# A decode step of attention and a gated unit on one core: the last V piece, the gate product and the weight pieces cut differently

## The chip, the core and the metric

The kernel runs on one core of one Trainium2 chip. The metric is device time in microseconds (us) of one execution. The engines are TensorE (PE, with its weight loads PEld), VectorE (DVE), ScalarE (ACT), GpSimd (POOL) and SyncE (SP); SP issues nearly all transfers, which 16 DMA engines carry out.

## What is computed

One token goes through a pre-norm attention with a cache and then through a gated unit, each with its residual:

```python
def _A_ref(x, k_cache, v_cache, wq, wo):        # x: 1 x 1 x 512
    q = (x @ wq) -> 32 heads of 128
    # 8 heads of K and V, 65536 rows of 128 each, shared by 4 heads of q
    p = softmax(q . k * 128 ** -0.5)
    return (p . v) -> 4096 values, @ wo          # 4096 x 512
def _B_ref(x, w_gate, w_up, w_down):             # 512 x 1792, 512 x 1792, 1792 x 512
    h = sigmoid(x @ w_gate) * (x @ w_up)
    return h @ w_down
h   = x + _A_ref(layernorm(x), ...)
out = h + _B_ref(layernorm(h), ...)
```

Everything is bf16. K and V are 134 MB each, the weights 14 MB.

## The kernel before

**Storage.** A ring in SBUF (`ring`) holds 32 chunks; a chunk is 16 rows of the cache per partition, 512 KB over 128 partitions. A head's K or V (32 chunks) is loaded in three pieces of 12, 8 and 12 chunks (`PIECES`, L228), each by one transfer on SP's queue (`load`, L323). Later the ring also takes w_gate, w_up and w_down (`AT`, L230). `ktw` holds transposed K and, at the end, the output weights wo.

**The loop over heads.** For each of 8 heads there are four blocks of 8 chunks. DVE transposes the chunks of K (L511), PE multiplies them with the query (scores, L430), DVE takes maxima, ACT takes exponentials (L557), and DVE transposes the result (L567). The sums over V of the head before run on PE between the scores: 16 rounds of eight matmuls (two chunks of V, four column tiles each; `pv`, L587, also L430), all adding into one PSUM bank (`PO`). Then ACT copies the bank out (L600), PE and ACT bring it into columns (L603, L606).

**How the order is made.** The engines' instruction lists are written out by hand with named dependencies (`Prog.op`, `Prog.dma`); a wait stands ahead of the instruction that needs it. PE's list is not unrolled. `pe_flow` (L669) is a small program of registers and branches. `sums` (label at L712, body L731 to L736) is one round of the V sums: `pv_regs` (L577) works out the addresses of the eight matmuls in registers, then eight matmuls follow, registers are moved on, and the counter `m` decides on another round. When `m` is 0 and `k` is not, PE jumps to the block `waits` (L718), which sets `m` to `k` and waits for the next V piece where one is due; from there it jumps back to `sums`. When both are 0, it goes on to `outs` (L740), the copy out. `away` (L672) writes a conditional jump to a block whose code stands behind the loop.

**The last head.** The V piece of chunks 20 to 31 comes in two transfers, chunks 20 to 27 and 28 to 31 (`LAST`, L318, L349). PE waits for the first (section V3, L711), runs four rounds, goes to `waits`, waits for the second (section VL, L729), and runs two rounds. While V's last pieces come in, PE works on wo for the first seven heads (`project7`, L636).

**The tail.** After the last head's copy out follow its part of wo (L632), a second layer norm (L804 to L811, hc at L805), 16 matmuls with w_gate and 16 with w_up (L818; four column tiles of 448 columns, four steps over the rows), tanh on ACT (L825), `sg2` on DVE (L826), the gate product `hh` (L828), its transpose `hhT` (L831), and 56 small matmuls with w_down: 14 rows of four column tiles (L836). Row r needs columns 32r to 32r + 31 of `hhT`. Two copies each on DVE and ACT (L842, L844) and one store (L846) end the kernel.

**Transfers of the tail.** SP issues, in this order: the last head's V pieces, w_gate in one piece (it waits for the first six rounds of the last head, since it lies where those chunks of V were), w_up in two (three steps of rows, then one; L316, L355), w_down in three (rows 0 to 7, 8 to 11, 12 to 13; L235, L360). Each piece has its own semaphore, and PE waits for it at its first matmul.

## Time and profile before

| | |
|---|---|
| median of 3 runs | 657.5 us (657.47 to 658.03) |
| the profiled execution | 657.62 us |
| its span in the profile | 656.2 us |
| PE busy | 436.0 us (66%) |
| DVE busy | 351.2 us (54%) |
| ACT busy | 42.8 us (7%) |
| read from memory | 282.33 MB, 430 GB/s over the span |
| granted TensorE clock, mean | 0.775 |

How to read it: the span is the time from the first to the last instruction that the profiler recorded; the execution's own time is 1.4 us longer. Busy times of engines overlap each other. A row of the timeline gives start and length in us, the engine, the line of the code, the operation, what it writes and reads, how many instructions were merged, and in brackets how long the engine had been idle before and who released it. "issue" is time in which the engine waited for nothing that the profile shows, and PEq is PE's sequencer, which also runs registers, branches and waits.

### The profile page before, as it was taken

To read this page: it belongs to the slowest core of one execution; us is meant where nothing else is said; L and a number is where in the kernel's file an instruction comes from. 1 tells how busy PE (TensorE), PEld (TensorE's weight loads), DVE (VectorE), ACT (ScalarE), POOL (GpSimd) and SP (SyncE) were. 2 spreads that over 40 slices of the span, in tenths; PEclk is the share of its full clock that TensorE was granted. 3 is DMA by queue.
4 is the path that set the end of the run, shared out by engine and by line. 5 is a ranking of instruction groups with operands and counts; after the bars stand their busy time and mean duration, and the time that the engine had idled before them with its cause. 6 is when DMAs were issued, how large, how long until landed. Compare 5 with 4: busy or idle time off the path is not lost.

```text
span 656.2 us, 6248 instructions
## 1 busy us (share of the span) xinstructions
PE 436.0 (66%) x2316; PEld 69.4 (11%) x1548; DVE 351.2 (54%) x436; ACT 42.8 (7%) x114; POOL 3.6 (1%) x17
## 2 busy tenths in 40 slices
PE   2698675838658457776676477594667856775855
PEld 1100010001001010010100110010100101001212
DVE  3498836847266645647258380674536572573102
ACT  1100200020000200011000200002000020002001
POOL 1000000000000000000000000000000000000000
PEclk9798688767689587796677676985877967877777
DMA  9999999999999999999999999999999999999998
GB/s 400 431 447 431 425 424 446 437 434 426 441 431 431 431 431 442 437 434 423 423 443 431 431 437 445 437 437 431 415 431 431 431 434 434 457 431 411 439 422 341
DMA packets 8386, 282.33 MB, mean 430 GB/s; under 512 B 961, under 2 KB 962, under 8 KB 1474
## 3 DMA queue, kind: packets, MB, share of 16 engines
q1 hardware_dynamic: 8354, 282.33, 99.6%
q10 hardware_dynamic: 32, 0.00, 0.0%
HBM read 282.33 MB, written 0.00 MB: 430 GB/s over the span
## 4 chain that ended last, share of the span: by engine, by line
DMA 65%; PE 19%; DVE 12%; issue 3%; ACT 1%; SPq 0%; PEldq 0%
DMA ring<-in_A_k_cache_dram 34%; DMA ring<-in_A_v_cache_dram 23%; PE PS L430 18%; DVE ktw L511 11%; DMA ring<-in_B_w_down_dram 6%; DMA ring<-in_A_wq_dram 2%; ACT P_sb L557 1%; DVE PT_sb L567 0%; DVE M_sb L518 0%; SPq L355 0%; PE PS L551 0%; PE PS L544 0%; PEldq L171 0%; SPq L360 0%; PE PS L572 0%
## 5 line engine op out<-in xcount | busy, mean ns | idle before, releaser
L511 DVE STREAM_TRANSPOSE ktw<-ring 128x1024 f32<-128x1024 f32 x256 | 292.4, 1211 | 170.5 <-DMA ring<-in_A_k_cache_dram 170.5
L430 PE MATMUL PS<-ktw 128*128 128x512 bf16 x1024 | 293.2, 438 | 114.8 <-DVE ktw L511 106.7
L430 PE MATMUL PS<-ring,PT_sb 128*32 x1024 | 102.7, 506 | 65.4 <-PEq L171 45.1
L430 PEld LDWEIGHTS PS<-ktw 128*128 x256 | 27.2, 106 | 370.4 <-issue 258.1
L600 ACT ACTIVATE po_sb<-PS,rl 128x512 bf16<-128x512 f32 x8 | 5.5, 687 | 522.2 <-PE PS L430 522.2
L430 PEld LDWEIGHTS PS<-ring,PT_sb 128*32 x1024 | 20.7, 116 | 144.3 <-issue 142.8
L518 DVE TENSOR_REDUCE M_sb<-PS 128x1 f32<-128x512 f32 x32 | 19.9, 684 | 20.0 <-PE PS L430 20.0
L546 DVE TENSOR_REDUCE gmj<-PS 1x4 f32<-1x128 f32 x8 | 2.2, 278 | 40.2 <-PE PS L544 40.2
L557 ACT ACTIVATE P_sb<-PS,negmax 128x512 bf16<-128x512 f32 x32 | 21.5, 685 | 0.3
L567 DVE STREAM_TRANSPOSE PT_sb<-P_sb 128x512 bf16<-128x512 bf16 x32 | 20.2, 688 | 1.7 <-ACT P_sb L557 1.7
L430 PE MATMUL PS<-ring,xz 128*8 x32 | 10.0, 490 | 3.6 <-DMA ring<-in_A_wq_dram 3.6
L616 DVE TENSOR_TENSOR Lw<-O,blk_of 128x896 bf16<-128x896 bf16 (+1 forms) x2 | 1.4, 682 | 19.9 <-ACT O L606 19.9
L544 PE MATMUL PS<-identf,gm 128*1 128x128 f32 x16 | 4.5, 380 | 5.5 <-issue 3.4
L551 PE MATMUL PS<-one_f,gmrep 1*128 1x1 f32 x16 | 4.7, 358 | 5.0 <-DVE gmrep L548 5.0
L574 DVE TENSOR_REDUCE lsum<-PS 128x1 f32<-128x4 f32 x8 | 1.3, 162 | 11.9 <-PE PS L572 11.9
L475 DVE STREAM_TRANSPOSE qt<-qh 32x512 bf16<-32x512 bf16 x1 | 0.7, 699 | 12.7 <-ACT qh L472 12.7
L430 PE MATMUL PS<-ktw,O 128*1 x26 | 7.5, 457 | 0.0
L557 ACT ACTIVATION_READ_ACCUMULATOR P_sb<-PS,negmax 128x1 f32 x32 | 6.5, 203 | 0.0
L603 PE MATMUL PS<-sel_bf,po_sb 128*128 128x4 bf16 x32 | 2.1, 170 | 6.3 <-ACT po_sb L600 6.3
L411 PE MATMUL PS<-xs,xpick 16*128 16x32 bf16 x1 | 0.2, 202 | 7.5 <-DMA xs<-in_A_x_dram 7.5
L572 PE MATMUL PS<-L_sb,lsel 128*128 128x4 f32 x16 | 2.5, 229 | 3.8 <-DVE PT_sb L567 3.8
L661 DVE COPY yr<-PS 1x512 f32<-1x512 f32 x1 | 0.7, 678 | 8.1 <-PE PS L659 8.1
(88 smaller groups left out, 71.6 us busy)
## 6 DMA issues: line engine op xcount, KB each, us to landing
ring<-in_A_k_cache_dram SPq DMA_DIRECT2D x16, 6144.0 KB, 25.4
ring<-in_A_v_cache_dram SPq DMA_DIRECT2D x15, 6144.0 KB, 25.7
ring<-in_A_v_cache_dram SPq DMA_DIRECT2D x9, 4096.0 KB, 30.6
ring<-in_A_k_cache_dram SPq DMA_DIRECT2D x8, 4096.0 KB, 24.7
ring<-in_A_wq_dram SPq DMA_DIRECT2D x1, 4096.0 KB, 12.3
ktw<-in_A_wo_dram SPq DMA_DIRECT2D x1, 3584.0 KB, 14.9
ring<-in_A_v_cache_dram SPq DMA_DIRECT2D x1, 2048.0 KB, 38.5
ring<-in_B_w_gate_dram SPq DMA_DIRECT2D x1, 1792.0 KB, 30.8
```

The lines of the kernel that those rows point to most:

```text
L430: return e.add_instruction(mybir.InstMatmult(name=nc.get_next_instruction_name(), engine=mybir.EngineType.PE, ins=[rhs, lhsT], outs=[e.low ...
L511: op("dve", lambda e, d=dst, sr=src: e.transpose(d, sr), deps, f"T{b}.{c}", to="T")
L518: op("dve", lambda e, u=u: e.tensor_reduce(M_sb[:, u % 4:u % 4 + 1], ps(u % NS, 0, 512), AX.X, ALU.max), [f"S{b}.{NC - NR + k}"], f"mx{u}" ...
L544: op("pe", lambda e: e.matmul(ps(MISC, 0, 128, 0, 1), lhsT=gm[:, :], rhs=identf[:, :], start=True, stop=True), [f"gm{h}"], f"gmT{h}", to="Q")
L546: op("dve", lambda e: e.tensor_reduce(gmj[:, :], ps(MISC, 0, 128, 0, 1).rearrange("p (i a c) -> p a i c", a=4, c=NC), AX.XY, ALU.max), [f" ...
L551: op("pe", lambda e: e.matmul(ps(MISC, 128, 129), lhsT=gmrep[0:1, :], rhs=one_f[0:1, 0:1], start=True, stop=True), [f"gmrep{h}"], f"neg{h}")
L557: op("act", lambda e, b=b: e.activation(P_sb[:, (b % 4) * 512:(b % 4 + 1) * 512], ps(b % NS, 0, 512), AF.Exp, bias=negmax[:, k:k + 1], sca ...
L567: op("dve", lambda e, b=b: e.transpose(PT_sb[:, (b % 4) * 512:(b % 4 + 1) * 512], P_sb[:, (b % 4) * 512:(b % 4 + 1) * 512]), [f"E{b}"], f" ...
L572: op("pe", lambda e: e.matmul(ps(MISC, 132, 136), lhsT=lsel[:, :], rhs=L_sb[:, :], start=True, stop=True), [f"PT{NR * h + NR - 1}"], f"l{h ...
L600: op("act", lambda e: e.activation(po_sb[:, :], ps(PO, 0, 512), AF.Copy, scale=rl[:, :]), [f"PV{h}.{NR - 1}", f"rl{h}"], f"po{h}", to="po")
L603: op("pe", lambda e, t=t: e.matmul(ps(OX, 0, 4), lhsT=po_sb[:, t * 128:(t + 1) * 128], rhs=sel_bf[:, 8 * t:8 * t + 8:2], start=(t == 0), s ...
L616: op("dve", lambda e: e.tensor_tensor(Lw[i][:, :].rearrange("p (j c) -> p j c", j=n), bass.AP(tensor=O2, offset=j0, ap=[[NQ, 128], [1, n], ...
```

## The change

Four things are cut differently.

1. V's chunks 28 to 31 of the last head come in two transfers, 28 to 29 and 30 to 31. PE runs four rounds, waits for 28 to 29, runs one round in the loop, comes to `waits` again, waits for 30 to 31, and runs the last round (`pv_last`) with its eight matmuls written out at fixed addresses. From there it jumps to `outs`.
2. w_up comes in one transfer, not two.
3. The gate product and its transpose are done in two parts, for rows 0 to 7 and 8 to 13 of w_down (columns 0 to 255 and 256 to 447).
4. w_down's three transfers have 8, 5 and 1 rows, not 8, 4 and 2.

```diff
-    WD_SPLIT = [(0, 8), (8, 12), (12, 14)]
+    WD_SPLIT = [(0, 8), (8, 13), (13, 14)]
...
-        W_SPLIT = {"wg": [(0, 4)], "wu": [(0, 3), (3, 4)]}
+        W_SPLIT = {"wg": [(0, 4)], "wu": [(0, 4)]}
-        LAST = [(20, 28), (28, 32)]
+        LAST = [(20, 28), (28, 30), (30, 32)]
...
-            load("V", h, 2, (), ("vb", "vl")[i], f"V{h}.2{('', 'b')[i]}", cols)
+            load("V", h, 2, (), ("vb", "vl", "vn")[i], f"V{h}.2{('', 'b', 'c')[i]}", cols)
...
+        def pv_last():
+            for n in (15,):
+                for k in range(2):
+                    for tq in range(4):
+                        lhsT = bass.AP(tensor=PT_sb, offset=(2 * (n % 2) + k) * 512 + 128 * tq + n // 2, ap=[[PT_ROW, 128], [4, 32]])
+                        at = (2 * n + k + first_chunk("V", HKV - 1, 2) - PIECES[2][0]) * CH + 4 * tq * DH
+                        op("pe", lambda e, tq=tq, lhsT=lhsT, at=at: e.matmul(
+                            ps(PO, 0, 512, 32 * tq, 32 * tq + 32), lhsT=lhsT, rhs=ring[:, at:at + 512], start=False, stop=False,
+                            tile_position=(0, 32 * tq), skip_group_check=True),
+                           (), f"PV{HKV - 1}.{NR - 1}" if n == 15 and k and tq == 3 else None)
...
                 label("last_rounds", "fourth")
+                e.br_ne(m, 1, on_true="last_but_one", on_false="last_round")
+                label("last_but_one", "last_rounds")
+                e.reg_mov(m, 1)
+                e.reg_mov(k, 1)
                 section("VL")
+                nc.br("sums", engines=here)
+                label("last_round", "last_rounds")
+                section("VM")
...
-            away("br_ne", k, 0, "waits", waits, "sums")
-
-            away("br_eq", w, w0 - 12, "outs", lambda: section("O"))
+            away("br_ne", k, 0, "waits", waits, "outs")
+
+            away("br_eq", w, w0 - 12, "outs", lambda: section("O"), under="sums_end")
...
                     if last:
+                        pv(i - 1, r, 4, "a")
                         P.part["pe"] = ("VL", i)
                         op("pe", lambda e: None, [f"V{i - 1}.2b"])
-                    pv(i - 1, r)
+                        pv(i - 1, r, 1, "b")
+                        P.part["pe"] = ("VM", i)
+                        op("pe", lambda e: None, [f"V{i - 1}.2c"])
+                        pv_last()
+                    else:
+                        pv(i - 1, r)
...
-        op("dve", lambda e: e.tensor_tensor(hh[:, :].rearrange("p (r q) -> p r q", r=NF),
-                                            ps(UB, 0, FG).rearrange("p (q r) -> p r q", r=NF),
-                                            sg2[:, :].rearrange("p (q r) -> p r q", r=NF), ALU.mult), ["gu1", "sg2"], "hh")
-        op("dve", lambda e: e.transpose(hhT[:, :], hh[:, :]), ["hh"], "hhT")
+        HH = ((0, 8), (8, NF))
+        for i, (r0, r1) in enumerate(HH):
+            op("dve", lambda e, r0=r0, r1=r1: e.tensor_tensor(
+                hh[:, 32 * r0:32 * r1].rearrange("p (r q) -> p r q", q=32),
+                ps(UB, 0, FG).rearrange("p (q r) -> p r q", r=NF)[:, r0:r1, :],
+                sg2[:, :].rearrange("p (q r) -> p r q", r=NF)[:, r0:r1, :], ALU.mult), ["gu1", "sg2"], f"hh{i}")
+            op("dve", lambda e, r0=r0, r1=r1: e.transpose(hhT[:, 32 * r0:32 * r1], hh[:, 32 * r0:32 * r1]), [f"hh{i}"], f"hhT{i}")
...
-                       ["hhT", f"wd{i}"] if r == r0 and g == 0 else (), "y" if last else None)
+                       ([f"wd{i}"] if r == r0 and g == 0 else []) + [f"hhT{j}" for j, (h0, _) in enumerate(HH) if r == h0 and g == 0], "y" if last else None)
```

More of the change, by code (lines that the diff above doesn't have):

```diff
@@ L585, in bass_sequential_preLN__gqa_block_cached__glu_gated_glu__decode_kernel, with pv @@
         PARTS = {0: 10, 3: 6}
-        def pv(h, r, rounds=0):
+        def pv_last():
[8 more added lines that the diff above has]
+                           (), f"PV{HKV - 1}.{NR - 1}" if n == 15 and k and tq == 3 else None)
+        def pv(h, r, rounds=0, part=""):
             P.part["pe"] = ("B", (h, r, rounds))
-            rounds, name = rounds or PARTS[r], f"PV{h}.{r}" + "a" * (rounds == 6)
+            rounds, name = rounds or PARTS[r], f"PV{h}.{r}{part}"
             for k in range(2):
@@ L670, in pe_flow, with away @@
             later = []
-            def away(op, reg_, value, name, body, back=None):
+            def away(op, reg_, value, name, body, back=None, under=None):
                 getattr(e, op)(reg_, value, on_true=name, on_false=f"{name}_not")
-                later.append((name, body, back or f"{name}_not", blocks[-1][0]))
-                label(f"{name}_not")
+                later.append((name, body, back or f"{name}_not", under or blocks[-1][0]))
+                label(f"{name}_not", under)
             i, w, p, v, m, k, s = (R.setdefault(n, e.alloc_register(f"r_{n}")) for n in "iwpvmks")
@@ L779, in bass_sequential_preLN__gqa_block_cached__glu_gated_glu__decode_kernel @@
                     if last:
-                        pv(i - 1, r, 6)
+                        pv(i - 1, r, 6, "a")
                     P.part["pe"] = ("L" if last else "V2", i)
```

## The prediction

> **What bounds the kernel now.** I read three things in this order: the page's strip of DMA shares with its list of queues, the end of the chain of waits, and the timeline of the last 20 us. All times are microseconds from the span's start unless another unit stands beside them.

> The page first, with the DMA share in 40 slices and then packets, MB and share of 16 engines' span for each queue:

> ```profile
> DMA  9999999999999999999999999999999999999998
> ...
> q1 hardware_dynamic: 8354, 282.33, 99.6%
> q10 hardware_dynamic: 32, 0.00, 0.0%
> ```

> No slice but the last is below nine tenths: the 16 DMA engines are full from start to end, and TensorE (66%) and VectorE (54%) are not. So 282.33 MB set the time, and only what follows the last byte can be shortened. The chain of waits (start, length, what) says where that byte hands over:

> ```profile
> 616.72 37.16 DMA ring<-in_B_w_down_dram
> 653.88 0.04 issue
> 653.92 0.41 PE PS L836 x7
> ```

> The last w_down piece lands at 653.88, its eight products run, and the result's copies and store fill the rest of the 656.2 us span. Landing times of the other pieces follow from the transfers (KB, us from issue to landing):

> ```profile
> ring<-in_A_v_cache_dram SPq DMA_DIRECT2D x1, 2048.0 KB, 38.5
> ...
> ring<-in_B_w_down_dram SPq DMA_DIRECT2D x1, 512.0 KB, 37.0
> ring<-in_B_w_up_dram SPq DMA_DIRECT2D x1, 448.0 KB, 34.3
> ring<-in_B_w_down_dram SPq DMA_DIRECT2D x1, 256.0 KB, 37.2
> ```

> The chain lists SP's issues one by one: w_up's second part starts at 615.29, w_down's second at 616.24. So they land at 615.29 + 34.3 = 649.6 and 616.24 + 37.0 = 653.2. The last V piece is the third of three issues that fill 1.38 us from 601.48, so it starts about 602.4 and lands at 641.0.

> The timeline of the end (start, length, engine, line, instruction, count, idle before and releaser) shows the second strand, the work between the last V piece and w_down:

> ```profile
> 636.76 3.82 PE L430 MATMUL PS<-ring,PT_sb 128*32 x32 [6.04 <-PEq L171]
> ...
> 641.68 0.63 PE L430 MATMUL PS<-ring,PT_sb 128*32 x8 [1.10 <-DMA ring<-in_A_v_cache_dram]
> ...
> 642.65 0.63 PE L430 MATMUL PS<-ring,PT_sb 128*32 x8 [0.34 <-issue]
> 643.33 0.69 ACT L600 ACTIVATE po_sb<-PS,rl 128x512 bf16<-128x512 f32 x1 [36.40 <-PE PS L430]
> ...
> 650.74 0.92 DVE L828 TENSOR_TENSOR hh<-PS,sg 128x448 bf16<-128x448 f32 x1 [0.31 <-PE PS L818]
> 651.69 0.65 DVE L831 STREAM_TRANSPOSE hhT<-hh 128x448 bf16<-128x448 bf16 x1
> ...
> 652.39 0.62 PE L836 MATMUL PS<-ring,hhT 128*1 128x128 bf16 x32 [1.29 <-DVE hhT L831]
> 653.29 0.39 PE L836 MATMUL PS<-ring,hhT 128*1 128x128 bf16 x16 [0.29 <-DMA ring<-in_B_w_down_dram]
> 653.92 0.38 PE L836 MATMUL PS<-ring,hhT 128*1 128x128 bf16 x8 [0.23 <-DMA ring<-in_B_w_down_dram]
> ```

> The reader is to see two things. PE waits for w_down twice at the end, so the arithmetic strand is early there. And the wait at 641.68 is put down to a transfer that had landed at 641.0; the strand was really in its branches, as the next rows show.

> **The change part by part.**

> *Transfers.* Bytes and pieces stay the same: V's last 2048 KB becomes 2 x 1024, w_up's 1344 + 448 becomes 1792, w_down's 512 + 256 becomes 640 + 128. SP issues one V piece more ahead of w_gate's wait (released near 614.4) and one w_up piece less behind it; each issue took about 0.45 us, and w_gate's bytes move only after the V piece lands at 641, so some 26 us of queue hide it. The trace's packet records (one per partition) give 84 ns for 2048 B, 140 for 3584, 159 for 4096, 309 for 8192, 404 for 10752, 535 for 14336, 611 for 16384, and 47 for the 1024 B of the result. Between the rows for 4096 and 8192, 5120 B is 159 + 150/4 = 197. Before: 611 + 404 + 140 + 159 + 84 = 1398 ns; after: 2 x 309 + 535 + 197 + 47 = 1397. Eight packets per engine make that 0.01 us. The last byte still lands at 653.88; w_down's second part one row (128 KB at the page's 430 GB/s, 0.30) later, 653.5.

> *V's last rounds.* Today, after four rounds, PE's sequencer goes through the loop's exit to the block with the waits and back. The rows of the branches (min/median/max ns):

> ```profile
> L736 PEldq COMPARE_BRANCH  x128: 78/214/216, 83.7 to 643.0; - x128
> L721 PEldq COMPARE_BRANCH  x16: 72/140/208, 89.7 to 640.7; - x16
> ```

> A branch not taken costs 72 to 78 ns, one taken 207 to 216; in the sequencer's records the next instruction starts some 55 ns after, so 0.13 and 0.27. The exit runs from 640.04 (L736, not taken) over two moves, two taken branches and one not taken to the wait at 641.07, already after the landing at 641.0; then back (0.24), address registers (0.37), first matmul at 641.68. The change makes PE do this twice. First pass: one more compare (0.13) and two moves (0.19): round 15 starts at 642.00 instead of 641.68, although its piece landed at 641.0 - 2.4 = 638.5. Second pass: compare of the loop 0.33 after the first matmul, not taken (0.13), exit branch taken (0.27), two moves (0.24), branch taken (0.27), one not taken (0.13), the new one taken (0.27): the eight matmuls at fixed addresses start at 643.65, not 642.65. Fixed addresses save the 0.37 of registers; the second detour costs more. V's sum ends **1.0 us later**, 644.3. The jump straight to the output block lies beside ACT's 0.69 us copy. All that follows shifts by 1.0 until w_up.

> *w_up in one piece.* Today the gate products start at 647.59 and w_up's follow without a gap; all 32 take 3.09. Shifted, w_up's 16 start at 650.1. The single piece lands with today's second part, 649.6, so it is hidden by 0.5, thanks to V being late; without that lateness it would have cost 0.5. The product hh starts at 650.74 + 1.0 = 651.74.

> *Gate product and transpose in two.* Prices lie between proportional (nothing fixed) and a fixed part of 0.16 per instruction, which the 128x4 and 128x1 VectorE rows show. The product (0.92 for 448 columns) is then 0.52 to 0.59 for 256 and 0.39 to 0.48 for 192; the transpose (0.65) 0.37 to 0.44 and 0.28 to 0.37, or up to 0.52 and 0.47 by the slope to the 128x512 transpose (0.69). With three gaps of 0.03 the four take 1.65 to 2.15; I take the fixed 0.16, the nearest small rows: 1.97. The second transpose ends at **653.7** (653.4 to 653.9), the first at 652.8, so rows 0 to 7 (0.62) are done before it.

> *w_down.* Rows 8 to 12 start at 653.76; a row's four matmuls follow each other every 0.055 (the starts from 652.39 on in the records). Row 13 starts at 654.03 and ends 0.27 later: 654.30. Today the last matmul ends at 654.30 too. With a faster split, row 13 waits for the landing, starts at 653.92 and ends at 654.19 (-0.11, the one row less after the last byte); with a slow one 654.5 (+0.2). Copies (0.59) and store stay.

> The sum: **0.0 us**, bounds -0.11 and +0.2. The profiled execution took 657.62 around its span of 656.2; the median of the runs is 657.50, 0.12 lower, and they spread from 657.47 to 658.03. So 657.5. I call anything within 0.2% (1.3 us) the same, which is about what a measurement of this kernel can tell from no change.

> [...]

> **Rivals.**

> *The strand becomes the bound* (slower, small). It has no cover left: what comes on top goes into the end one for one. For it: the granted clock was 0.50 in 644 to 647 and 0.56 in 647 to 651, and the last matmuls stretched from 219 to 314 ns. A third detour's worth (1.0) gives 658.5. Against it: every step is priced from rows of this strand.

> *A stop at the new blocks* (slower, over 0.2%). The last round's code stands in a block of its own, reached by a jump; were its code fetched only then, the fetch would queue behind full DMA engines. The nearest row is the 1 KB load of x on its own queue beside q1: 6.7 us from issue to landing. It would decide as soon as it takes over 1.3 us; at 6.7 the time is 664.2. Against it: the page lists only q1 and q10 (8354 + 32 of 8386 packets), so nothing was fetched in the span, and all taken branches cost alike. [...]

> *The split does what it is meant to do* (faster). If PE reached the last wait before the landing at 641.0, V's sum would end by 641.7 and the strand be 1.6 early. Then w_up's landing would hold it (649.6, hh at 651.2), and the end is again the last byte: 654.19, 657.4. Faster than 656.2 in all needs the stream itself to be shorter, for which no row speaks.

> **How the numbers follow.** Forecast, level within 0.2 of 657.5: 0.67. Strand late by 0.2 to 1.3: 0.12; by more: 0.05. A stop at new code: 0.06. Early strand, 657.4: 0.05. A shorter stream, below 656.2: 0.05. Same is 0.67 + 0.12 + 0.05 = 0.84, slower 0.11, faster 0.05. The range leaves out the last two outer cases: from 657.0 (-0.11 and the spread of builds) to 658.6 (the strand 1.0 late).

> **What would show it.** Right: V's last eight matmuls near 643.7 (wrong, if before 642); the first w_up matmul near 650.1 with no wait for its transfer; second transpose ending 653.4 to 653.9; DMA still at 99% and the last landing at 653.9. Wrong above all if the last landing moves, or a gap over 1.5 us stands ahead of V's last round.

## The result, and the profile after

The changed kernel takes **659.29 us** (median of 10 runs, 659.15 to 660.92) against 657.53 (657.45 to 658.53): slower by 1.76, ratio 1.0027 with a 95% interval of 1.0017 to 1.0036. The forecast was 657.5 in a range to 658.6. The profiled execution took 659.76 around a span of 658.4, 2.2 longer than before.

The page of the changed kernel, list of queues (packets, MB, share of 16 engines' span), has a line that the page of before does not have:

```profile
q1 hardware_dynamic: 8354, 282.33, 99.3%
q8 instruction: 1, 0.02, 0.0%
q10 hardware_dynamic: 32, 0.00, 0.0%
```

One packet of instructions, 16 KB, came in during the span. The data packets are as many as before. The packet records put it at 619.96, for 0.93, while PE ran the loop over wo's rows (615.98 to 621.92) and did not stop. The transfers (KB, us from issue to landing) show what it did:

```profile
ring<-in_A_v_cache_dram SPq DMA_DIRECT2D x2, 1024.0 KB, 38.8
...
ring<-in_B_w_up_dram SPq DMA_DIRECT2D x1, 1792.0 KB, 36.0
...
ring<-in_B_w_down_dram SPq DMA_DIRECT2D x1, 128.0 KB, 38.9
```

Before, w_down's last part needed 37.2 and w_up's 34.3. By the records of the landings, the piece that ends at 616.7 lands as before (616.74 and 616.75). Of the next piece 15 engines deliver at 626.05 to 626.43, and the sixteenth at 627.87, where before all were in by 626.48. The records of landings do not name the engines, but in every later piece too one of the 16 comes 1.3 to 1.4 behind the other fifteen. Counted to the last of the 16, V's last piece lands at 642.39 (before 640.97), w_up at 650.86 (649.58), w_down's last row at 655.21 (653.88), so all of them are 1.3 to 1.4 late.

The timeline of the end (start, length, engine, line, instruction, count, idle before and releaser), same steps as shown for before:

```profile
638.08 3.88 PE L430 MATMUL PS<-ring,PT_sb 128*32 x32 [5.43 <-PEq L171]
...
643.37 0.63 PE L430 MATMUL PS<-ring,PT_sb 128*32 x8 [1.41 <-issue]
...
645.00 1.05 PE L593 MATMUL PS<-ring,PT_sb 128*32 128x512 bf16 x8 [1.00 <-issue]
...
650.36 3.15 PE L842 MATMUL PS<-ring,hc 128*1 128x448 bf16 x32 [0.26 <-DVE hc L829]
...
653.57 0.59 DVE L854 TENSOR_TENSOR hh<-PS,sg 128x256 bf16<-128x256 f32 x1 [0.37 <-PE PS L842]
654.19 0.45 DVE L858 STREAM_TRANSPOSE hhT<-hh 128x256 bf16<-128x256 bf16 x1
654.56 0.43 DVE L854 TENSOR_TENSOR hh<-PS,sg 128x192 bf16<-128x192 f32 x1
...
654.78 1.66 PE L863 MATMUL PS<-ring,hhT 128*1 128x128 bf16 x56 [0.54 <-DVE hhT L858]
655.03 0.38 DVE L858 STREAM_TRANSPOSE hhT<-hh 128x192 bf16<-128x192 bf16 x1
```

The reader is to see a shift of 1.32 in the first line (636.76 before), two idle stretches ended by "issue" around the single round at 643.37, where PE's sequencer goes twice through the loop's exit (the two pieces had landed at 639.97 and 642.39), and 56 products with w_down in one row without a wait. The strand of arithmetic ends last, not a transfer; the end of the chain of waits (start, length, what) says the same:

```profile
654.78 1.69 PE PS L863 x56
656.48 0.02 issue
656.50 0.09 DVE y_sb L869
```

V's sum ends at 646.05 instead of 643.28, 2.77 late. The lines give the parts: 1.32 the landing; 5.29 instead of 4.92 from the first of the four rounds to the next one, 0.37; 1.63 instead of 0.97 to the last one, 0.66; and 1.05 instead of 0.63 for the last round, 0.42, at a granted clock of 0.51 (before, both single rounds ran at 1.00, 641 to 643). The windows view of the changed kernel shows that clock and that of the last products (stretch and length; busy time of PE, PEld, DVE, ACT and POOL; granted clock; DMA share and GB/s):

```profile
645.00:647.00 2.00, 1.21 (x12) 0.31 (x12) 0.00 (x0) 0.69 (x1) 0.00 (x0) 0.51 1.05 452
...
655.00:656.50 1.50, 1.45 (x56) 1.15 (x44) 0.38 (x2) 0.00 (x1) 0.00 (x0) 0.50 0.00 0
```

### The profile page after: what moved, and what is told of

It is laid out like the page before. It is cut to its first block, busy times and chain, and to the rows that moved or that the text cites. A ratio compares the mean times of both kernels' runs of the same rounds, so it can differ in the third digit from the quotient of the medians.

```text
span 658.4 us, 6251 instructions
## 1 busy us (share of the span) xinstructions
PE 432.1 (66%) x2316; PEld 68.7 (10%) x1548; DVE 351.7 (53%) x438; ACT 42.8 (7%) x114; POOL 3.6 (1%) x17
## 3 DMA queue, kind: packets, MB, share of 16 engines
q1 hardware_dynamic: 8354, 282.33, 99.3%
HBM read 282.33 MB, written 0.00 MB: 429 GB/s over the span
## 5 line engine op out<-in xcount | busy, mean ns | idle before, releaser
L430 PE MATMUL PS<-ktw 128*128 128x512 bf16 x1024 | 292.8, 436 | 115.9 <-DVE ktw L511 108.2
L430 PE MATMUL PS<-ring,PT_sb 128*32 x1016 | 100.2, 498 | 71.0 <-PEq L171 44.4
L430 PEld LDWEIGHTS PS<-ktw 128*128 x256 | 27.0, 106 | 371.8 <-issue 262.2
L430 PEld LDWEIGHTS PS<-ring,PT_sb 128*32 x1016 | 20.5, 116 | 147.1 <-issue 145.7
L430 PE MATMUL PS<-ring,xz 128*8 x32 | 9.0, 452 | 3.6 <-DMA ring<-in_A_wq_dram 3.6
L430 PE MATMUL PS<-ktw,O 128*1 x26 | 5.9, 378 | 0.0
L553 ACT ACTIVATE negmax<-PS 128x1 f32<-128x1 f32 x8 | 1.4, 172 | 56.1 <-PE PS L551 56.1
```

Of the source, the lines that this page charges most:

```text
L430: return e.add_instruction(mybir.InstMatmult(name=nc.get_next_instruction_name(), engine=mybir.EngineType.PE, ins=[rhs, lhsT], outs=[e.low ...
L553: op("act", lambda e: e.activation(negmax[:, k:k + 1], ps(MISC, 128, 129), AF.Copy, scale=-att_scale), [f"neg{h}"], f"negmax{h}")
```

## The experiments

Theory A: the added code makes PE's program longer, a further block of instructions is fetched while the 16 DMA engines are full, and the engine that carries it sets all later landings. Theory B: V's second detour on PE. Theory C: the new cuts of the transfers cost DMA time. PE's compiled program has 476 instructions before and 498 after.

**1. Only the length of the code.** The kernel before with a block that is never entered. Five lengths were tried: with 3, 5, 7, 9 and 137 in place of the 9 below, PE's program has 486, 490, 494, 498 and 754 instructions.

```diff
             label("more_heads")
+
+            def never_run():
+                for _ in range(9):
+                    e.reg_alu(s, s, 3, ALU.add)
+                    e.reg_alu(s, s, 5, ALU.bitwise_xor)
+
+            away("br_eq", i, 0, "never_run", never_run)
```

> The kernel before, with 18 register instructions in a block of PE's program that is never entered (a compare that is never true leads there, once per head, not in the last one). PE's compiled program grows from 476 to 498 instructions, the size of the changed kernel; nothing else differs. Theory A (the added code makes PE's sequencer fetch one more block of instructions in the span, and the DMA engine that carries it falls behind by about 1.3 us, so that all later pieces land late): one instruction packet of 16 KB near 620 us, the last w_down piece lands near 655.2 instead of 653.9, and the time is 658.7 to 659.0. Theory B (V's second detour and nothing else) and theory C (the new cuts of the transfers cost DMA time): no packet, no shift, 657.5.

Measured with 498: 658.83 (658.38 to 660.12) against 657.64; ratio 1.0019 (1.0009 to 1.0028). The page lists one packet on q8, and the chain of waits still ends on the transfer, only later:

```profile
617.25 37.79 DMA ring<-in_B_w_down_dram
655.03 0.04 issue
655.08 0.31 PE PS L843 x8
```

So 22 instructions, 18 of them never run, cost 1.19: theory A, with the arithmetic of before. The packet stands at 621.00, and the time and the landing are as expected.

> The padded kernel before with 6 instructions that are never run: 486 instructions on PE, between 483 (no packet) and 490 (a packet at 656.1, after the last data, and times in two groups, 658.4 to 658.8 and 660.2 to 661.6). Theory A': a program under the border brings no packet and takes 657.5. If the border lies under 486: a packet after the last data and 658.4 to 661.6, as with 490. If the compare in each head costs time: more than 657.8 without a packet.

Measured with 486: 657.60 against 657.61, ratio 1.0002 (0.9992 to 1.0011), no packet. The compare in each head costs nothing that this interval shows.

> The same padding with 10 instructions that are never run: 490 instructions on PE. It lies between the largest program seen without a packet (483) and the smallest with one (497). Theory A: either no packet, the last landing at 653.9 to 654.1 and 657.5, or a packet, the last landing near 655.1 and 658.8; nothing in between. Rival (the compare in each head costs the time): 658.8 without a packet.

> The same with 14 such instructions: 494 instructions on PE, between 490 (packet after the data) and 497 (packet in the span, near 620). Theory A': the packet is asked for when PE comes within a fixed distance of the next block, so that it stands either in the span near 620 with all later landings 1.2 to 1.4 late and 658.8, or at the end as with 490, 658.4 to 661.6; no time under 658.

Measured: 490 gives 660.59 against 657.61, in two groups (658.35 to 658.81 and 660.23 to 661.55), ratio 1.0036 (1.0023 to 1.0048); 494 gives 659.09 (658.70 to 659.40), ratio 1.0022 (1.0012 to 1.0031). The packet is there, but at 656.09 and 655.64, after the last data; the last piece lands as before at 653.94 and 653.66. The page's first line with 494:

```profile
span 656.2 us, 6256 instructions
```

That execution took 659.40: the span is that of before, and 3.2 lie around it instead of 1.4. In all 20 executions of these two versions 2.2 to 5.3 lie around the span; for the kernel before it is 1.3 to 1.6 in most, at most 2.5. So this is a third outcome, which the expectation for 490 did not have and the one for 494 had as its second case. In both profiles the packet ends after the span (from 656.09 for 0.93, and from 655.64 for 1.24), but that the program's end waited for it is not shown: no run separates it from other work around the span. The border for any packet lies between 486 and 490.

> [...] Theory A (each block of PE's program that comes in during the span costs one DMA engine about 1.2): two instruction packets; 660.0 if one engine carries both, 658.8 if two engines carry one each, since the end waits for the slowest engine alone; over 662 if PE itself has to stand still for a block. Rival (length as such costs nothing, the 1.2 came from the compare that was added in each head): one packet or none and 658.8.

Measured with 754, which is 256 more than 498: 659.92 (659.70 to 661.03), ratio 1.0041 (1.0027 to 1.0055). Two packets, as expected; the expectation of a second one was the author's estimate, since no run shows how many instructions a packet holds. They stand at 618.47 and 626.01, and two engines fall behind: of the piece whose engines else end by 626.4, one delivers at 627.56 and one at 628.01. The last landing is 655.21, as with one packet. What is new is that PE stands still, in the middle of seven matmuls (timeline of this run, PE):

```profile
614.76 0.43 PE L622 MATMUL PS<-row_of,Lw 128*128 128x4 bf16 x5 [0.83 <-issue]
...
620.74 0.27 PE L622 MATMUL PS<-row_of,Lw 128*128 128x4 bf16 x2 [5.55 <-issue]
...
639.59 3.75 PE L430 MATMUL PS<-ring,PT_sb 128*32 x32 [3.67 <-PEq L171]
```

The landings bear out the expectation for two engines: two that are late cost no more than one. The time does not; it lies 1.1 above the 658.8 of that case and well under the 662 of a stop. The rows say why: PE stood still for 5.55, most of which fell into the pause that it had anyway, but V's four rounds begin at 639.59, 1.7 later than with 498 (637.91). In this run the strand of arithmetic ends last, not a transfer.

**2. V's part alone** (the changed kernel with w_up, w_down and the gate product as before).

```diff
-    WD_SPLIT = [(0, 8), (8, 13), (13, 14)]
+    WD_SPLIT = [(0, 8), (8, 12), (12, 14)]
...
-        W_SPLIT = {"wg": [(0, 4)], "wu": [(0, 4)]}
+        W_SPLIT = {"wg": [(0, 4)], "wu": [(0, 3), (3, 4)]}
...
-        HH = ((0, 8), (8, NF))
+        HH = ((0, NF),)
```

> V's last piece in two, its last round at fixed addresses, with w_up, w_down and the gate product as before; 497 instructions on PE. Theory A with B: the instruction packet is there, V's later pieces land 1.3 late, V's sum ends 2.4 to 2.8 late, the undivided product and transpose follow, and the end is set by the strand of arithmetic: 659.3 to 660.0. Theory C: the shift of the landings stays away, since w_up and w_down are cut as before; 658.3 to 658.7 by the strand alone.

Measured: 659.62 (659.17 to 659.96) against 657.64, ratio 1.0027 (1.0017 to 1.0037), the packet at 619.78, last landing 655.04, the strand last. V's sum ends at 645.57, 2.29 late, just under the 2.4 expected. V's part alone loses as much as the whole change.

**3. The other three parts alone** (the diff of the change without its V lines).

> The other three parts alone: w_up in one piece, product and transpose in two, w_down in 8, 5 and 1 rows; V as before; 477 instructions on PE. Theories A and B: no instruction packet, last landing at 653.9; w_up's 16 products start at its landing, 649.6, 0.5 later than in the kernel before, the second transpose ends near 653.1 and the last row waits for its landing: 657.4. Theory C: the last landing moves by up to 1.3, 657.8 to 658.9.

Measured: 657.49 (657.28 to 658.64) against 657.64, ratio 1.0000 (0.9991 to 1.0009). No packet, last landing 653.99. The timeline:

```profile
649.75 1.66 PE L818 MATMUL PS<-ring,hc 128*1 128x448 bf16 x16 [0.32 <-DMA ring<-in_B_w_up_dram]
...
653.70 0.57 PE L839 MATMUL PS<-ring,hhT 128*1 128x128 bf16 x24 [0.40 <-DMA ring<-in_B_w_down_dram]
```

PE waits for w_up's single piece, and in the end for w_down again. Theory C falls: these cuts neither cost nor gain anything beyond the interval.

**4. The changed kernel without the packet.** First, the last round back in the loop (483 instructions):

```diff
-            away("br_ne", k, 0, "waits", waits, "outs")
+            away("br_ne", k, 0, "waits", waits, "sums")
...
-                        pv_last()
+                        pv(i - 1, r, 1)
```

> The changed kernel, but the last round goes back into the loop with its register addresses instead of eight matmuls at fixed addresses; 483 instructions on PE. Theory A: if 483 lie below the border of a block, no instruction packet, the last landing at 653.9, and the time is V's second detour (1.0, and 0.4 for the registers) with the lower clock on top of it: 658.0 to 658.6; if above, the packet is there and the time is 659.3 to 659.8. Theory B: 659.3 or more whether or not there is a packet.

Measured: 658.60 (658.21 to 659.17) against 657.64, ratio 1.0014 (1.0005 to 1.0023). No packet, last landing 654.06, and the strand ends last: what two detours with register addresses cost without the packet, 0.96, at the upper edge of what was expected. Both single rounds took 1.05 here too, at a clock of 0.50 (641 to 645). Second, all of the change kept and other code left out (467 instructions; `yr`, which that code fills, is set to zero at the start instead):

```diff
                     if last:
-                        project7()
                         columns()
```

> The changed kernel without the product of the first seven heads with wo (its part of the output is left out; the matmuls stand in PE's pause between V's sums, 615 to 624): 467 instructions on PE. The second detour, the fixed addresses and all cuts of the transfers stay. Theory A: no packet, the last landing at 653.9 to 654.1, the strand 1.3 earlier than in the changed kernel: 658.0 to 658.4, what the detour costs alone. Theory B alone (no part for the packet): 659.3.

Measured: 657.93 (657.40 to 658.37) against 657.61, ratio 1.0003 (0.9994 to 1.0012). No packet, last landing 653.93. So without the packet the change costs 0.32, within the interval, and most of the 1.76 is gone. This run also leaves out PE work in 615 to 624, well before V's last pieces. Its strand shows where the packet acted (compare the rows of the changed kernel above):

```profile
636.74 4.01 PE L430 MATMUL PS<-ring,PT_sb 128*32 x32 [5.61 <-PEq L171]
...
653.66 0.38 DVE L857 STREAM_TRANSPOSE hhT<-hh 128x192 bf16<-128x192 bf16 x1
...
654.18 0.51 PE L862 MATMUL PS<-ring,hhT 128*1 128x128 bf16 x24 [0.16 <-DVE hhT L857]
```

The four rounds start 1.34 earlier and the second transpose ends 1.37 earlier (654.04 against 655.41), as much as the landing of V. The last product ends 1.76 earlier (654.69 against 656.45): the 0.4 beyond that come with the clock of the last products, 1.00 here in 653 to 655 and 0.50 there in 655 to 656.5.

**5. The packet without the second detour** (508 instructions): both last rounds at fixed addresses, one behind the other.

```diff
...
-                e.br_ne(m, 1, on_true="last_but_one", on_false="last_round")
...
                 section("VL")
-                nc.br("sums", engines=here)
-                label("last_round", "last_rounds")
                 section("VM")
...
-                        pv(i - 1, r, 1, "b")
+                        pv_last(14)
...
-                        pv_last()
+                        pv_last(15)
```

> The changed kernel with both of V's last rounds at fixed addresses, one behind the other, each with its wait, and no way back through the loop: 508 instructions on PE. The packet stays, the second detour goes. Theory A with B: landings 1.3 late as in the changed kernel, V's sum ends about 1.9 earlier than there (two exits of the loop become one, and the address registers of one round go), hh starts near 651.7, the last row waits for its landing near 655.2: 658.6 to 658.8, 0.6 below the changed kernel. If the detours cost nothing of the end: 659.3.

Measured: 658.99 (658.68 to 659.14) against 657.61, ratio 1.0020 (1.0011 to 1.0029); packet at 618.65, last landing 655.12. V's sum ends 2.1 earlier than in the changed kernel, and only 0.3 of it reaches the time, half of what was expected. The chain of waits ends on a landing, that of rows 8 to 12 of w_down at 654.79; the 24 products behind it took 0.84, at a clock of 0.50, where the two runs of experiment 4 took 0.53 at 1.00.

No version measured beats the kernel before beyond its interval.

## Why the prediction was wrong

- **"The last byte still lands at 653.88": wrong, and this is the step that failed.** It landed at 655.21, and the prediction had itself named a last landing that moves as the first sign of being wrong. The packets of data were counted rightly (8354 in both). What was left out is the packet of code: put on the kernel before, alone, it cost 1.19 and took the time to 658.83, past the range's 658.6. The rival "A stop at the new blocks" was set aside because the page of *before* lists no instruction packet. That page speaks for 476 instructions, not for 498; a cost that begins between 486 and 490 instructions cannot be read from a trace with 476. It was also priced as a stop of PE at 6.7. In the changed kernel PE did not stop; a DMA engine fell 1.3 to 1.4 behind, and with it V's rounds as well as the last landing.
- **V's sum 1.0 later through the detours: right.** The two detours took 0.37 + 0.66 = 1.03. **The last round itself was mis-sized:** it was put at its old length and took 0.42 more, at a clock of 0.51. So V's sum ended 2.77 late: 1.32, 1.03 and 0.42.
- **w_up hidden: right.** Its products follow the gate's without a gap (3.15 for 32).
- **Second transpose 1.97 after hh's start: 1.84 measured** (653.57 to 655.41), within the bounds. Products 0.59 and 0.43, transposes 0.45 and 0.38. Its end was late by what came before it: 653.4 to 653.9 forecast, 655.41 measured.
- **A row of w_down every 0.055: mis-sized too.** By the starts in the records a row followed the other every 0.107, at a granted clock of 0.50 (655.0 to 656.5). The 0.055 came from rows at a clock of 1.00. After the second transpose 1.04 passed to the end of the last product, not 0.59. It is not what put the strand last: in the prediction's own sum the strand ended last too (row 13 at 654.03, behind its landing), and here the second transpose ended at 655.41, after the last landing.
- **The strand has "no cover left: what comes on top goes into the end one for one": right,** and with it the rival that it belongs to, whose reason was the clock. In the profiled execution the last product ended at 656.45, 2.15 after the forecast 654.30, and the rows add up to it: 1.32 the landing, 0.03 the detours, 0.42 the last round, 0.06 the gate's and w_up's products, 0.13 less for product and transpose, 0.45 w_down's products. The span grew by as much.
- **The rest of the sum was sound.** Without the packet (467 instructions) the two single rounds start at 641.97 and 643.61 (forecast 642.00 and 643.65), and the last product ends at 654.69, 0.39 after the forecast; the last round's clock accounts for 0.42.

How the 1.76 divides: about 1.4 goes with the packet (659.29 with it, 657.93 without it, each with its own kernel before: 1.76 and 0.32), and the 0.32 that stays is within the interval. The other runs give 1.19 (code alone), 1.38 (packet without the second detour) and 0.96 (detours without the packet, with register addresses). They do not add up exactly, since the end waits for the later of the two strands, and since the clock differs between the runs: about 0.9 of the 2.15 in the profiled execution (0.42 and 0.45 of its parts) is slow clock. That execution took 0.47 more than the median, so the median may hold less of it. Whether the packet brings the low clock at the end is open; the padded kernel with 498 has the packet and a clock of 1.00 in 653 to 655.

## What to carry to other kernels

Here the DMA engines were busy for 99% of the span, and the version with one packet of 16 KB of code took 1.19 more (experiment 1, 498 instructions): look for an instruction row among the queues, know how many instructions each engine's program has, and keep it below the border at which a further packet comes (here between 486 and 490 instructions on PE; another program's border has to be found). A wait that seems to be for a transfer may be time in the sequencer's branches (before, PE's wait for V ended at 641.68, 0.71 after the landing at 640.97); compare it with the transfer's landing before splitting the transfer. One small packet can delay everything behind it: in the changed kernel one of the 16 engines came 1.3 to 1.4 behind in every later piece, and PE's steps from V's sum on came late with it.
